# Attention and two feed-forward layers on one core: values by pairs of units, scores of both blocks in one group, sinks placed by VectorE, weight splits held back

## The chip, the cores and the metric

The kernel runs on one core of one Trainium2 chip. The metric is the device time of one execution in microseconds (us), the median of three runs. Engines are named as in the profile: PE is TensorE's matmul side, PEld its weight loads, DVE VectorE, ACT ScalarE, POOL GpSimd, and SP the queue that issues DMAs.

## The reference, cut to what matters

```python
# q, k, v: 2 batches, 8 heads, 768 positions, head size 64, float32; n_sink 4, window 128
scores = scale * np.matmul(q, k.transpose(0, 1, 3, 2))
keep = is_sink | in_window            # the first 4 keys, and the 128 last ones up to the query
a = softmax(np.where(keep, scores, -1e9))
x = np.matmul(a, v)                   # -> 1536 tokens x 512
h = x @ w_in;  x = np.maximum(0.01 * h, h) @ w_out                # 512 -> 2048 -> 512
h = x @ w_in2; x = (h * (1.0 / (1.0 + np.exp(-h)))) @ w_out2      # 512 -> 2048 -> 512
```

## The kernel before

**Attention.** A *unit* is 256 queries (`GT`, a group G) of one pair of heads p; there are 6 groups of 4 units, 24 units, and every unit has two *blocks* of 128 queries, i = 0 and 1. One block of one unit is a *slot*. The groups run in the order of `in_turn`: first the two that begin a sequence (g = 0, units 0 to 7), then the other four (g > 0, units 8 to 23). In the first three groups (units 0 to 11, `whole`) the score matmuls are float32 with a contraction of 64, and the two heads j sit on the upper and the lower half of the array; in the others q and k are cut into float32r parts (`qkh`, `ql`) and the contraction is 128. For a slot, `scores` makes the scores in the PSUM tile `sc`, adds the mask and takes the maximum on DVE (listed as CUSTOM_DVE or ISA, out `P`), and exponentiates on ACT. `normalise` makes the reciprocal of the sum; in units 0 to 7 it builds a scaled identity `by`, in the others it scales `P`. `transposes` turns `P` over on PE (`tr`, or `h` for some) and copies it with ACT into `pT`. With g > 0 the four sink columns go through `psink` (copied by ACT as high part, low part by DVE, and high part again by ACT), are transposed on PE into columns 256 to 383 of the tile `at`, and two ACT copies of 32 rows each (`sink_t<-at`) place them. `values` then multiplies by v (`at<-pT,v`, output of 64 rows for each head) and adds the sinks (`at<-sink_t,sk`); ACT and DVE write the parts `xh` and `xl`.

**Feed-forward.** Each layer has 16 chunks of 128 hidden columns. An *item* is one chunk for some tokens: `emit_h` (12 matmuls into `h`), the nonlinearity on ACT and DVE (`ga`, `gb`, each as a high and a low part), and `emit_y` two items later (`ya` of 256 columns, `y` of 512). While attention runs, 30 items of 256 tokens run beside it; from about 185 us on only items of 512 tokens are left.

**Weights.** Each half of a chunk comes as 64-bit numbers (`wr`, 512 KB) and is made into a high and a low float32r part by two ACT and five DVE instructions (`load_half`: tiles `wb`, then `w` or `we`).

**Order.** All instructions are recorded as operations, and `Recorder.order` places them by a list schedule: durations come from `cost`, and of the operations that could start first the one with the earliest due time is taken. `either` leaves the engine of an operation open; `scaled` could go to ACT, DVE or POOL. Each engine then executes its own row of instructions in the order so written. All engine work is recorded at one source line, so the rows of the profile are told apart by tile names.

Of the kernel before, what the change touches and what calls it, by code (L numbers as in the profile page):

```python
# [36 lines left out]
W_FIRST, W_EVERY = 1, 1.3  # L37

# [8 lines left out]
def f32(ap):  # L47
    return ap.bitcast(F32)


class View:
# [28 lines left out]

    def size(self):
        n = 1
        for a, b in self.box[1:]:
            n *= b - a
        return n
# [28 lines left out]
class Op:  # L114
    def __init__(self, eng, rank):
        self.eng, self.rank = eng, rank
        self.calls, self.cost, self.deps, self.opens, self.users = [], 0, {}, [], []
        self.bytes, self.port, self.mode = 0, False, None

        self.alts = {}  # L120


class Recorder:
# [7 lines left out]
    def __init__(self, tc):  # L131
# [3 lines left out]
        self.after = None  # L135
        for e in self.ENGINES:
            setattr(self, e, _Engine(self, e))
# [13 lines left out]
    def cost(self, eng, name, out, ins, kw):  # L151
        n = out.size() if isinstance(out, View) else 0
        psum = any(isinstance(a, View) and a.tile.pool.psum for a in [out, *ins])
        if eng == "tensor":
            passes = 4 if ins[0].dtype == F32 else 1

            half = name == "matmul" and min(out.box[0][1] - out.box[0][0], ins[0].box[0][1] - ins[0].box[0][0]) <= 64
            if name == "transpose":
                return max(109, n / 2.4)
            return n * passes / 2.4 * (0.5 if half else 1) + (20 if half else 13.3)  # L160
        if name == "dma_start":
            return 0
        if eng == "scalar":
            by = any(isinstance(kw.get(k), View) for k in ("scale", "bias"))
            sparse = isinstance(ins[0], View) and ins[0].tile.tag == "wr"
            return (182 if by else 51 if psum else 93) + n / 1.2 + (95 if "accum_out" in kw else 55 if sparse else 0)
        if eng == "vector":
# [3 lines left out]
            if name == "reciprocal":  # L171
                return 70 + n * 6
            return 68 + n / (0.96 if two or psum else 1.92)
# [15 lines left out]
    def add(self, eng, name, args, kw):  # L189
# [111 lines left out]
    def order(self):  # L301

        for op in self.ops:
            op.need, op.est = len(op.deps), 0.0
            for d in op.deps:
                d.users.append(op)
        self.deadlines()
        free = dict.fromkeys(self.ENGINES, 700.0)
# [43 lines left out]
        while len(done) < len(self.ops):  # L352
# [33 lines left out]
            else:  # L386
                end = free[op.eng] = start + op.cost
                if op.eng == "tensor":

                    end = free[op.eng] = end + (95 if mode is not None and mode != op.mode else 0)  # L390
# [65 lines left out]
def attention_moe(ctx, tc, cfg, ins, out):  # L456
# [35 lines left out]
    def load_half(after=None):  # L492
# [5 lines left out]
        R.after = after  # L498
# [16 lines left out]
        R.after = None  # L515
# [32 lines left out]
    def emit_y(yps, gt, t, layer, c, first, last):  # L548
        cs = slice(c * P, (c + 1) * P)
        with R.group():  # L550
            for j, (a, b) in enumerate(((0, 0), (1, 0), (0, 1))):
                l, r = (wo(t, a)[:, cs], gt[:, b, :]) if layer == 0 else (gt[:, b, cs], wo(t, a))
# [4 lines left out]
    if near:  # L557
        mask = [attn.tile([P, 260], BF16, f"mask{i}") for i in range(4)]
        psink = [attn.tile([P, P], F32, f"psink{i}") for i in range(2)]
        sink_t = [attn.tile([P, GT], F32R, f"sink_t{i}") for i in range(2)]  # L560

# [40 lines left out]
    def load_qk(n):  # L602
# [19 lines left out]
        R.gpsimd.tensor_tensor(ql, raw[:, :, :GT], f32(hi[:, :, :GT]), op=ALU.subtract)  # L622
# [4 lines left out]
    def load_v(n):  # L627
# [7 lines left out]
        if d["g"] > 0 and key not in sinks:  # L635
            sr = attn.tile([P, P + 1], F32, "sr", 2)
            R.sync.dma_start(out=sr, in_=ins["vs"][key])

            sh = attn.tile([P, P], F32R, "sh", 1)
            R.vector.tensor_copy(sh, sr[:, :P])  # L640
            sinks[key] = attn.tile([P, P], F32R, "sk", NP + 1)
            R.vector.scalar_tensor_tensor(sinks[key], in0=f32(sh), scalar=sr[:, P:P + 1], in1=sr[:, :P],
# [5 lines left out]
    def scores(s):  # L648
# [10 lines left out]
        scs = {}  # L659
        if u["whole"]:  # L660

            scs = {j: ps_a.tile([P, 260], F32, "sc", 2) for j in range(2)}
            with R.group():
                for j, sc in scs.items():
# [3 lines left out]
        for j in range(2):  # L668
            if j in scs:
                sc = scs[j]  # L670
            else:
                sc = ps_a.tile([P, 260], F32, "sc", 2)
# [10 lines left out]
    def normalise(s):  # L683
# [5 lines left out]
        if d["u"]["whole"] and d["g"] == 0:  # L689

            d["by"] = attn.tile([P, 2, P], F32, "by", 3)
# [6 lines left out]
        if d["g"] > 0:  # L698
            s0 = 2 * P if i == 0 else P
            src = pt[:, :, s0:s0 + NS]  # L700
            hi, lo, hi2 = (psink[s // 2 % 2][:, o:o + 2 * NS].rearrange("p (j s) -> p j s", j=2)
                           for o in range(32 * i, 32 * i + 6 * NS, 2 * NS))
            R.scalar.activation(hi.bitcast(F32R), src, AF.Copy)
            R.vector.tensor_tensor(lo.bitcast(F32R), src, hi, op=ALU.subtract)
            R.scalar.activation(hi2, hi, AF.Copy)
        R.bias = 0

    def transposes(s):
# [16 lines left out]
        if i == 0:  # L725
            u["pT"] = attn.tile([P, 2, 512], F32, "pT", 2)
# [5 lines left out]
        u["at"] = ps.tile([P, 512], F32, "ya0", 1) if early and s // 2 % 2 else ps_a.tile([P, 512], F32, "at", 1)  # L732
        if g > 0:

            R.tensor.transpose(u["at"][:, 256:384], psink[s // 2 % 2], ident)
            st = u["st"] = sink_t[s // 2 % 2]
            for k in range(2):
                r = slice(32 * k, 32 * k + 32)
                R.scalar.activation(st[r, k * QB:(k + 1) * QB], u["at"][r, 256:384], AF.Copy)

    def values(n):

        u = state.pop(n)
        g, av, v, pT = u["g"], u["at"], u["v"], u["pT"]
        mm = [(1, 128, 384, 0), (0, 0, 128, 0), (2, 384, 512, 128)] if g > 0 else [(0, 128, 384, 0), (1, 384, 512, 128)]
        with R.group():
            if g > 0:
                R.tensor.matmul(av[:, 0:GT], sinks[u["G"] // NG, u["p"]], u["st"], start=True, stop=False)
            for k, (blk, a, e, o) in enumerate(mm):
                for j in range(2):  # L750
                    r = slice(D * j, D * j + D)
                    R.tensor.matmul(av[r, o:o + e - a], v[:, blk, r], pT[:, j, a:e],
                                    start=g == 0 and k == 0, stop=k == len(mm) - 1)
        T, t0 = divmod(u["G"] * GT, 512)
        x = [t[T][:, u["p"], t0:t0 + GT] for t in (xh, xl)]
        R.scalar.activation(x[0], av[:, 0:GT], AF.Copy)
# [294 lines left out]
```

## Time and profile before

| | us |
|---|---|
| median of three runs (lowest, highest) | 629.14 (628.79, 629.53) |
| the profiled execution, its own time | 629.62 |
| span of that execution, first to last instruction | 627.8 |
| PE busy in the span | 616.7 |
| DVE busy | 400.7 |
| ACT busy | 320.7 |
| POOL busy | 29.4 |

The span is what the views below divide up; the execution's own time is 1.8 us longer than its span. A busy PE is not yet PE at its peak, since matmuls are pipelined and their ends are modelled: where PE is compared with itself, the distance between the starts of two rows is used. A matmul in float32 shows as two rows.

### The profile page before, as it was taken

How to read it: one execution, taken by the hardware profiler on the slowest of the kernel's cores; microseconds unless marked ns; L12 is line 12 of the kernel's file. 1: busy time of each engine (PE TensorE's matmuls, PEld its weight loads, DVE VectorE, ACT ScalarE, POOL GpSimd, SP SyncE). 2: the span in 40 equal slices, each digit the busy share in tenths (PEclk: the TensorE clock that was granted, in tenths of full speed). 3: DMA queues.
4: the chain of work that ended last, by engine and by line, in shares of the span. 5: the costliest groups of instructions: out<-in, count | busy, mean ns of one | idle time of the engine just before them, and what ended most of it. 6: DMA issues, size and time to landing. Idle time of an engine off the chain costs nothing.

```text
span 627.8 us, 9200 instructions
## 1 busy us (share of the span) xinstructions
PE 616.7 (98%) x3368; PEld 518.8 (83%) x3368; DVE 400.7 (64%) x984; ACT 320.7 (51%) x789; POOL 29.4 (5%) x44
## 2 busy tenths in 40 slices
PE   7899999999999999999999999999999999999997
PEld 5688888989998888888888888888888888888886
DVE  4998978788696666443646498874554644455254
ACT  5989999999764333332434256454323323332221
POOL 2002013320000000000000000000000000000000
PEclk9999999999999999999999999999999999999999
DMA  8544654331253212020010113220101010000013
GB/s 297 155 167 160 207 173 140 124 102 47 83 190 130 75 62 102 33 68 33 34 66 34 38 66 135 101 101 33 65 4 68 34 34 33 1 0 1 2 67 134
DMA packets 19341, 53.34 MB, mean 85 GB/s; under 512 B 2144, under 2 KB 6752, under 8 KB 19296
## 3 DMA queue, kind: packets, MB, share of 16 engines
q1 hardware_dynamic: 19296, 52.76, 24.6%
q8 instruction: 26, 0.43, 0.3%
q14 instruction: 19, 0.16, 0.1%
HBM read 49.61 MB, written 3.15 MB: 84 GB/s over the span
## 4 chain that ended last, share of the span: by engine, by line
PE 87%; ACT 10%; DVE 2%; issue 1%; DMA 0%; DVEq 0%; ACTq 0%
PE h L441 40%; PE y L441 35%; PE ya L441 5%; ACT P L441 4%; PE sc L441 3%; PE tr L441 2%; PE at L441 2%; ACT pT L441 2%; ACT qkh L441 1%; DVE P L441 1%; ACT psink L441 1%; ACT sink_t L441 1%; ACT ga L441 0%; ACT xh L441 0%; DMA qk<-in_qkd 0%
## 5 line engine op out<-in xcount | busy, mean ns | idle before, releaser
L441 PE MATMUL h<-xh,w 128*128 128x512 f32 (+1 forms) x600 | 157.2, 350 | 0.0
L441 ACT ACTIVATE g<-h 128x512 f32<-128x512 f32 (+1 forms) x111 | 59.6, 537 | 138.5 <-PE h L441 138.5
L441 PEld LDWEIGHTS h<-xh,w 128*128 128x128 f32 x600 | 104.7, 189 | 14.7 <-issue 0.8
L441 DVE TENSOR_TENSOR gb<-g,gb 128x512 fp32r<-128x512 f32 x81 | 55.9, 690 | 77.0 <-ACT g L441 61.2
L441 PE MATMUL h<-xl,w 128*128 128x512 f32 (+1 forms) x300 | 104.0, 347 | 0.0
L441 DVE TENSOR_TENSOR g<-g,h 128x512 f32<-128x512 f32 x48 | 33.0, 687 | 91.6 <-ACT g L441 91.6
L441 DVE SCALAR_TENSOR_TENSOR wb<-wr,wb 128x512 uint32<-128x512 uint32 x128 | 87.7, 689 | 2.8
L441 PE MATMUL h<-xh,we 128*128 128x512 f32 x288 | 88.7, 389 | 0.0
L441 ACT ACTIVATE gb<-h 128x512 fp32r<-128x512 f32 x33 | 19.7, 597 | 100.9 <-PE h L441 100.9
L441 PE MATMUL y<-we,gb 128*128 128x512 f32 x288 | 69.2, 389 | 0.0
L441 PE MATMUL y<-w,gb 128*128 128x512 f32 x288 | 68.9, 389 | 0.0
L441 PEld LDWEIGHTS y<-w,gb 128*128 128x128 f32 x288 | 54.1, 188 | 11.2
L441 PEld LDWEIGHTS y<-we,gb 128*128 128x128 f32 x288 | 54.1, 188 | 11.2
L441 PEld LDWEIGHTS h<-xh,we 128*128 128x128 f32 x288 | 54.1, 188 | 11.1
L441 PEld LDWEIGHTS h<-xl,w 128*128 128x128 f32 x300 | 56.7, 189 | 7.1
L441 ACT ACTIVATE P<-P,sm 128x260 f32<-128x260 f32 (+2 forms) x118 | 56.8, 492 | 7.5 <-DVE sm L441 7.3
L441 PE MATMUL y<-gb,w 128*128 128x512 f32 x252 | 60.5, 389 | 0.0
L441 PE MATMUL h<-xl,we 128*128 128x512 f32 x144 | 56.1, 390 | 0.0
L441 DVE TENSOR_SCALAR wb<-wb 128x512 f32<-128x512 f32 (+1 forms) x128 | 53.6, 424 | 3.6 <-ACT wb L441 2.2
L441 PEld LDWEIGHTS y<-gb,w 128*128 128x128 f32 x252 | 47.3, 188 | 9.8
L441 PE MATMUL ya<-ga,w 128*128 128x256 f32 x360 | 49.6, 286 | 0.0
L441 DVE TENSOR_TENSOR yp<-yp,y 128x512 f32<-128x512 f32 (+1 forms) x61 | 38.0, 673 | 14.7 <-PE y L441 14.7
(72 smaller groups left out, 767.4 us busy)
## 6 DMA issues: line engine op xcount, KB each, us to landing
wr<-in_w SPq DMA_DIRECT2D x64, 512.0 KB, 3.6
qk<-in_qkd SPq DMA_DIRECT2D x12, 644.0 KB, 3.9
v<-in_vd SPq DMA_DIRECT2D x16, 192.0 KB, 2.5
out_y<-yp SPq DMA_DIRECT2D x11, 256.0 KB, 2.1
qk<-in_qkd SPq DMA_DIRECT2D x4, 322.0 KB, 5.7
v<-in_vd SPq DMA_DIRECT2D x8, 128.0 KB, 3.5
qkh<-in_qkd SPq DMA_DIRECT2D x4, 256.0 KB, 6.7
qk<-in_qkd SPq DMA_DIRECT2D x3, 256.0 KB, 3.8
```

Of the source, the lines that this page charges most:

```text
L441: getattr(eng, name)(*[_real(x) for x in a], **{k: _real(x) for k, x in kw.items()})
```

## The change

1. `values` handles two units at once (`us`): their values and sinks stand in one bank `at` (256 columns each) as one uninterrupted group on PE, and `xh` and `xl` are written for both units by one ACT and one DVE instruction. The call moves from every unit to every second one.
2. In the two groups with g = 0, `scores` emits the score matmuls of both blocks of a unit as one group (unit 0 is left in two groups) into one bank for each head. Units 1, 3 and 5 use the bank `ya1` for one head.
3. The sinks are placed by one DVE product of the transposed sinks, read twice, with a 0/1 mask `own`, in place of two ACT copies; the high part goes into `psink` twice with one ACT instruction in place of two.
4. POOL makes masks only: `ql` goes to DVE, and `scaled` has ACT and DVE alone to choose from.
5. The operations of `load_half` may not be scheduled earlier than 16 us (`HOLD`) before their due time.
6. `cost` knows more cases (64-row matmuls, small outputs on ACT, scalars in SBUF on DVE, a slow start of PE, `COLD`), so the schedule is another one throughout.
7. For the last 512 tokens of layer two the last bank is cut into two halves of 256 columns in two banks, and the second half leaves by ACT's DMA queue.
8. Some tiles get other buffer counts: `pT` 3 in place of 2, `by` 2 in place of 3, `sr` 1 in place of 2.

```diff
+COLD = 11000
+HOLD = 16000.0
...
+            return n * passes / 2.4 * (0.5 if half else 1) + (95 if rows <= 64 else 20 if half else 13.3)
...
+            op.split = self.splitting and eng != "sync"
...
-                    ("vector", "tensor_scalar", (out, src, by, None), dict(op0=ALU.mult)),
-                    ("gpsimd", "tensor_scalar", (out, src, by, 1.0), dict(op0=ALU.mult, op1=ALU.mult)))
+                    ("vector", "tensor_scalar", (out, src, by, None), dict(op0=ALU.mult)))
...
+            op.est = max(0.0, op.due - HOLD) if op.split else 0.0
...
-        R.gpsimd.tensor_tensor(ql, raw[:, :, :GT], f32(hi[:, :, :GT]), op=ALU.subtract)
+        R.vector.tensor_tensor(ql, raw[:, :, :GT], f32(hi[:, :, :GT]), op=ALU.subtract)
...
+        if u["whole"] and g == 0:
+            if i == 0:
+                spare = {1: ["ya1", "sc"], 3: ["ya1", "sc"], 5: ["ya1", "sc"]}.get(s // 2, ["sc", "sc"])
+                u["sc"] = [ps_a.tile([P, 512], F32, t, 2) if t == "sc" else ps.tile([P, 512], F32, t, 1) for t in spare]
+            for blocks in ((i,),) if s < 2 else ((0, 1),) if i == 0 else ():
+                with R.group():
+                    for k in blocks:
+                        for j, sc in enumerate(u["sc"]):
+                            r = slice(D * j, D * j + D)
+                            R.tensor.matmul(sc[:, k * P:k * P + P * (k + 1)], u["raw"][r, k * QB:(k + 1) * QB],
+                                            u["raw"][r, GT:GT + P * (k + 1)], start=True, stop=True)
...
-            R.scalar.activation(hi.bitcast(F32R), src, AF.Copy)
+            R.scalar.activation(twice.bitcast(F32R), src.repeat(1, [P, 2, 2, NS]), AF.Copy)
             R.vector.tensor_tensor(lo.bitcast(F32R), src, hi, op=ALU.subtract)
-            R.scalar.activation(hi2, hi, AF.Copy)
...
-            for k in range(2):
-                r = slice(32 * k, 32 * k + 32)
-                R.scalar.activation(st[r, k * QB:(k + 1) * QB], u["at"][r, 256:384], AF.Copy)
+            R.vector.tensor_tensor(st.rearrange("p (k n) -> p k n", k=2), u["at"][:, o:o + P].repeat(1, [P, 2, QB]),
+                                   own.rearrange("p (k n) -> p k n", k=2), op=ALU.mult)
...
+        us = [state.pop(n + k) for k in range(2)]
...
             if g > 0:
-                R.tensor.matmul(av[:, 0:GT], sinks[u["G"] // NG, u["p"]], u["st"], start=True, stop=False)
+                for k, u in enumerate(us):
+                    R.tensor.matmul(av[:, k * GT:(k + 1) * GT], sinks[u["G"] // NG, u["p"]], u["st"],
+                                    start=k == 0, stop=False)
+            for k, u in enumerate(us):
+                for m, (blk, a, e, o) in enumerate(mm):
+                    o += k * GT
+                    for j in range(2):
+                        r = slice(D * j, D * j + D)
+                        R.tensor.matmul(av[r, o:o + e - a], u["v"][:, blk, r], u["pT"][:, j, a:e],
+                                        start=g == 0 and k == m == 0, stop=k == 1 and m == len(mm) - 1)
...
-        R.scalar.activation(x[0], av[:, 0:GT], AF.Copy)
-        R.vector.tensor_tensor(x[1], av[:, 0:GT], f32(x[0]), op=ALU.subtract)
+        both = av.rearrange("p (k n) -> p k n", k=2)
+        R.scalar.activation(x[0], both, AF.Copy)
+        R.vector.tensor_tensor(x[1], both, f32(x[0]), op=ALU.subtract)
...
-                values(b // 2 - 2)
+                if b % 4 == 2:
+                    values(b // 2 - 3)
...
+        ends = layer == 1 and final and T == NT - 1
+        parts = [(c, 0, 512) for c in range(KC - ends)] + ends * [(KC - 1, 0, 256), (KC - 1, 256, 512)]
...
+                (R.scalar if o else R.sync).dma_start(out=out[r0:r0 + P, cols], in_=part)
```

On PE's row of instructions, the stretch around the first values with sinks reads so before (two or three units of g > 0 are under way; `at` is the tile of one unit, and each `at<-pT,v` is 64 rows of output):

```order
L441 MATMUL ya_2_591<-ga_756,w_696 128x256 x6
L441 MATMUL ya_0_604<-ga_756,w_696 128x256 x6
L441 MATMUL at_844<-sink_t_0_129,sk_462 128x256
L441 MATMUL at_844<-pT_779,v_576 64x256 x2
L441 MATMUL at_844<-pT_779,v_576 64x128 x4
L441 MATMUL tr_932<-ident_88,P_753 128x128 x4
L441 MATMUL sc_941<-qk_92 128x260
L441 MATMUL sc_942<-qk_92 128x260
```

The same place of the changed program, where `at_787` is the tile of two units:

```order
L463 MATMUL at_787<-ident_88,psink_0_122 128x128
L463 MATMUL ya_2_904<-ga_817,w_276 128x256 x6
L463 MATMUL sc_916<-qk_92 128x260
L463 MATMUL sc_917<-qk_92 128x260
L463 MATMUL ya_4_924<-ga_817,w_276 128x256 x6
L463 MATMUL at_787<-sink_t_0_807,sk_306 128x256
L463 MATMUL at_787<-sink_t_0_909,sk_493 128x256
L463 MATMUL at_787<-pT_750,v_570 64x256 x2
L463 MATMUL at_787<-pT_750,v_570 64x128 x4
L463 MATMUL at_787<-pT_873,v_725 64x256 x2
L463 MATMUL at_787<-pT_873,v_725 64x128 x4
L463 MATMUL tr_969<-ident_88,P_835 128x128 x4
```

The values of the earlier unit have moved behind those of the later one, so the two runs of 64-row matmuls are one. Over the whole program there are 24 such runs before, 20 of them behind 128-row work and 4 behind scores, and 12 now, 9 and 3; runs of 64-deep score matmuls number 22 before and 15 now, and those that come behind 128-row work 17 and 14.

PE's row at the start, before (`sc` tiles of units 0 and 1, two for each block; `h_187` is a bank used for a transposition):

```order
L441 MATMUL sc_110<-qk_69 128x128
L441 MATMUL sc_111<-qk_69 128x128
L441 MATMUL sc_134<-qk_69 128x256
L441 MATMUL sc_135<-qk_69 128x256
L441 MATMUL sc_153<-qk_69 128x128
L441 MATMUL sc_154<-qk_69 128x128
L441 MATMUL tr_170<-by_159,P_122 128x128 x2
L441 MATMUL sc_181<-qk_69 128x256
L441 MATMUL sc_182<-qk_69 128x256
L441 MATMUL h_187<-by_176,P_144 128x128 x4
```

And in the changed program:

```order
L463 MATMUL sc_110<-qk_69 128x128
L463 MATMUL sc_111<-qk_69 128x128
L463 MATMUL sc_110<-qk_69 128x256
L463 MATMUL sc_111<-qk_69 128x256
L463 MATMUL ya_0_150<-qk_69 128x128
L463 MATMUL sc_151<-qk_69 128x128
L463 MATMUL ya_0_150<-qk_69 128x256
L463 MATMUL sc_151<-qk_69 128x256
L463 MATMUL tr_174<-by_161,P_131 128x128 x2
L463 MATMUL h_189<-by_170,P_143 128x128 x4
```

All scores of two units now stand ahead of the first transposition; the second block of unit 1 has moved up by one place.

DVE's row where the first unit with `ql` is prepared, in the changed program:

```order
L463 TENSOR_TENSOR qkh_828<-qk_69,qkh_828 64x2x388
L463 TENSOR_TENSOR psink_0_122<-P_771,psink_0_122 128x8
L463 TENSOR_TENSOR ql_878<-qk_69,qkh_828 128x512
L463 TENSOR_SCALAR wb_757<-wb_757 128x512
L463 TENSOR_SCALAR sm_836<-sm_836 128x2
L463 CAST sk_897<-sr_820 128x128
L463 ISA P_899,sm_900<-sc_881,mask_0_104 128x260
L463 ISA sm_900 128x1
L463 ISA P_899,sm_900<-sc_882,mask_0_104 128x260
L463 ISA sm_900 128x1
L463 TENSOR_TENSOR sink_t_0_909<-at_787,own_124 128x256
```

Before, neither the `ql` row nor the `sink_t` row stood on DVE; they are new there, 12 and 16 times in all. Counted over the program, DVE also has 43 scalings of `P` in place of 35, ACT 11 `by` in place of 7, and the 4 `by` and 7 scalings of POOL are gone. For the weights, the last half of a chunk is finished on DVE at least 3 items ahead of its first `h` from the 32nd item on; before, that lead was 5 items and more there.

## Rows read from the trace of the kernel before

**Rows 1.** The page: busy time by engine, and the chain that ended last.
```profile
PE 616.7 (98%) x3368; PEld 518.8 (83%) x3368; DVE 400.7 (64%) x984; ACT 320.7 (51%) x789; POOL 29.4 (5%) x44
...
PE 87%; ACT 10%; DVE 2%; issue 1%; DMA 0%; DVEq 0%; ACTq 0%
```

**Rows 2.** Busy time by stretch: length, then each engine with its instructions.
```profile
2.00:13.40 11.40, 9.37 (x36) 6.71 (x36) 5.79 (x38) 5.78 (x23) 2.36 (x12) 1.00 0.97 327
13.40:33.00 19.60, 17.90 (x140) 12.90 (x140) 18.88 (x86) 18.70 (x63) 1.53 (x4) 1.00 0.60 201
...
60.00:100.00 40.00, 39.28 (x334) 34.74 (x334) 34.51 (x133) 39.66 (x126) 7.64 (x6) 1.00 0.53 175
100.00:140.00 40.00, 39.18 (x334) 35.99 (x333) 31.68 (x115) 39.70 (x129) 13.62 (x11) 1.00 0.36 119
...
185.00:624.20 439.20, 439.20 (x1938) 363.67 (x1936) 247.57 (x415) 156.26 (x274) 0.00 (x0) 1.00 0.16 56
```

**Rows 3.** Waits of PE's weight loads, 33 to 185 us: total, times, longest.
```profile
PEld at L441 <- ACT sink_t L441: 1.6, 3, 0.7
PEld sc L441 <- DVE sm L441: 0.9, 2, 0.5
PEld at L441 <- ACT psink L441: 0.5, 1, 0.5
```

**Rows 4.** PE's timeline around the values of two units: start, length.
```profile
31.21 0.87 PE L441 MATMUL at<-pT,v 128*64 128x256 f32 x8
32.01 0.70 PE L441 MATMUL sc<-qkh 64*128 64x256 f32 x4
...
56.70 1.60 PE L441 MATMUL ya<-ga,w 128*128 128x256 f32 x12
58.14 0.28 PE L441 MATMUL at<-sink_t,sk 128*128 128x256 f32 x1
58.35 1.09 PE L441 MATMUL at<-pT,v 128*64 128x256 f32 x12
59.37 0.66 PE L441 MATMUL tr<-ident,P 128*128 128x128 f32 x4
```

**Rows 5.** Groups by line and shape: count, busy us, mean ns, idle before.
```profile
L441 DVE TENSOR_TENSOR gb<-g,gb 128x512 fp32r<-128x512 f32 x81 | 55.9, 690 | 77.0 <-ACT g L441 61.2 <-ACT gb L441 14.8
L441 POOL TENSOR_TENSOR ql<-qk,qkh 128x512 fp32r<-128x512 f32 x12 | 19.3, 1606 | 49.6 <-ACT qkh L441 39.0 <-issue 6.9 <-ACT psink L441 3.7
L441 DVE TENSOR_TENSOR qkh<-qk,qkh 64x776 fp32r<-64x776 f32 x12 | 13.5, 1127 | 1.7 <-ACT qkh L441 1.2
L441 DVE TENSOR_SCALAR P<-P,sm 128x260 f32<-128x260 f32 x35 | 11.7, 358 | 0.4
L441 DVE TENSOR_TENSOR xl<-at,xh 128x256 fp32r<-128x256 f32 x22 | 9.2, 420 | 3.0 <-ACT xh L441 2.7
L441 ACT ACTIVATE xh<-at 128x256 fp32r<-128x256 f32 x22 | 8.3, 377 | 0.7 <-PE at L441 0.7
L441 ACT ACTIVATE sink_t<-at 32x128 fp32r<-32x128 f32 x32 | 8.3, 259 | 0.2
L441 ACT ACTIVATE psink<-psink 128x8 f32<-128x8 f32 x32 | 5.9, 207 | 0.1
L441 ACT ACTIVATE by<-ident,sm 128x128 f32<-128x128 f32 x7 | 2.6, 392 | 0.1
```

**Rows 6.** The last DVE rows, on the timeline from 622 us.
```profile
624.25 0.75 DVE L441 TENSOR_TENSOR yp<-yp,y 128x256 f32<-128x256 f32 x2 [0.67 <-PE y L441]
```

**Rows 7.** DVE's timeline near 106 us.
```profile
106.37 0.96 DVE L441 TENSOR_TENSOR qkh<-qk,qkh 64x776 fp32r<-64x776 f32 x1
```

**Rows 8.** PE's timeline in the opening, 9 to 16 us.
```profile
9.63 2.08 PE L441 MATMUL h<-by,P 128*128 128x128 f32 x8
...
14.94 1.16 PE L441 MATMUL h<-by,P 128*128 128x128 f32 x8
```

**Rows 9.** The chain in order of time: its first work on PE.
```profile
3.20 0.85 PE sc L441 x4
```

More of the change, by code (lines that the diff above doesn't have):

```diff
@@ L135, in __init__ @@
         self.after = None
+        self.splitting = False
         for e in self.ENGINES:
@@ L172, in cost @@
                 return 70 + n * 6
+            if name == "tensor_scalar" and any(isinstance(a, View) for a in ins[1:]):
+                return 128 + n / 1.92
+            if two and not psum and out.box[0][1] - out.box[0][0] <= 64:
+                return 68 + n * 1.19
             return 68 + n / (0.96 if two or psum else 1.92)
@@ L388, in order @@
                 if op.eng == "tensor":
-                    end = free[op.eng] = end + (95 if mode is not None and mode != op.mode else 0)
+                    end += 95 if mode is not None and mode != op.mode else 0
+                    end = free[op.eng] = end + min(op.cost, max(0.0, COLD - start))
                     mode = op.mode
@@ L546, in emit_h, with emit_y @@
         R.vector.tensor_tensor(gt[:, 1, :], g, f32(gt[:, 0, :]), op=ALU.subtract)
-    def emit_y(yps, gt, t, layer, c, first, last):
+    def emit_y(yps, gt, t, layer, c, first, last, cols=slice(0, 512)):
         cs = slice(c * P, (c + 1) * P)
@@ L862, in attention_moe @@
                     R.gpsimd.memset(t, 0.0)
-                for t in sink_t:
-                    for k in (0, P):
-                        R.vector.tensor_copy(t[:, k:k + P], psink[0])
+                R.gpsimd.memset(own, 1.0)
+                for k in range(2):
+                    keep_where(own[:, k * QB:(k + 1) * QB], -32 * k, 1, 0, QB, 0.0)
+                    keep_where(own[:, k * QB:(k + 1) * QB], 32 * k + 31, -1, 0, QB, 0.0)
             while halves[0] < 2 * NA and b >= W_FIRST + halves[0] * W_EVERY:
@@ L922, in fused_h, with fused_y @@
         emit_h(fg[f], wt[c], layer, T, 0, 512)
[L924 removed]
+    def fused_y(f, banks=None):
         layer, c_w, T, first, last, new, final = items[f]
         gt = fg[f]
[L927 to L930 removed]
+        ends = layer == 1 and final and T == NT - 1
+        parts = [(c, 0, 512) for c in range(KC - ends)] + ends * [(KC - 1, 0, 256), (KC - 1, 256, 512)]
+        if first and banks in (None, [0]):
+            yps[:] = [ps.tile([P, 512], F32, "ya0", 1) if o else ps_y.tile([P, 512], F32, f"y{c}") for c, o, _ in parts]
+        for k in banks or range(len(parts)):
+            c, o, e = parts[k]
+            cols = slice(o, e)
+            yp_k = yps[k][:, :e - o]
+            emit_y(yp_k, gt, wt[c_w], layer, c, first, last, cols)
             if not last:
                 continue
[L933 removed]
+            part = yp[T][:, c, cols]
             if new:
[L935 removed]
+                R.scalar.activation(part, yp_k, AF.Copy)
             elif not final:
[L937 removed]
+                R.vector.tensor_tensor(part, part, yp_k, op=ALU.add)
             elif layer == 0:
[L939 removed]
+                R.vector.tensor_tensor(part, part, yp_k, op=ALU.add)
                 R.scalar.activation(xh[T][:, c, :], part, AF.Copy)
@@ L943, in fused_y @@
                 r0 = T * 512 + c * P
-                step = 256 if f == len(items) - 1 and c == KC - 1 else 512
-                for o in range(0, 512, step):
-                    e = slice(o, o + step)
-                    R.vector.tensor_tensor(part[:, e], part[:, e], yps[c][:, e], op=ALU.add)
-                    R.sync.dma_start(out=out[r0:r0 + P, e], in_=part[:, e])
+                R.vector.tensor_tensor(part, part, yp_k, op=ALU.add)
+                (R.scalar if o else R.sync).dma_start(out=out[r0:r0 + P, cols], in_=part)
     for f in range(len(items)):
@@ L956, in attention_moe @@
             fused_y(f - 2)
-    for c in range(KC):
+    for k in range(KC + 1):
         for f in (len(items) - 2, len(items) - 1):
-            fused_y(f, [c])
+            fused_y(f, [k])
     R.issue(ctx)
```

86 lines of the change are left out of this document (42 added, 44 removed).

## The prediction, made before the run

> **What bounds the kernel now.** I read the page first, for the engines' shares and the chain that ended last: PE is busy in 98% of the span and holds 87% of the chain, ACT 10% [rows 1]. So PE is the limit almost everywhere, and the question is where it isn't. The table by stretch answers that. From 185 to 624.2 us PE is busy without a gap, 439.2 of 439.2 us, and DVE and ACT are far from full (247.6 and 156.3) [rows 2]. Nothing can be won there that doesn't take matmuls away, and the change takes none away. In the attention stretch from 60 to 140 us PE is busy 78.5 of 80 us, but ACT is busy 79.4 of 80 and DVE 66.2 [rows 2]: PE and ACT are both full, and whatever ACT does late, PE waits for. The waits of the weight loads say for what: 1.6 us for the sink copies of ACT, 0.9 us for the softmax on DVE that frees the score banks, 0.5 us for the `psink` copies of ACT, 3.0 us in all between 33 and 185 us [rows 3]. Last comes the opening, where neither is full: 9.37 of 11.4 us of PE from 2 us on, then 17.9 of 19.6 [rows 2].
>
> A busy PE may still stand still inside a row, so I then looked at the distances between starts on PE's timeline. Twelve `ya` matmuls of 256 columns take from 56.70 to 58.14, so 0.12 us each. The sink matmul behind them has the same 256 columns, but the first 64-row matmul starts 0.21 us after it: going into the 64-row shape costs 0.09 us [rows 4]. The run of twelve rows lasts until 59.37, 1.02 us; the run of eight rows at 31.21 lasts 0.80 us until 32.01. The four extra rows are two 128-column matmuls and cost 0.22, 0.11 us each. A 256-column one is then 0.22, and the eight rows (two of each) should take 0.66; the missing 0.14 us goes into the first load in the new shape and the way out of it [rows 4]. So one run of values costs 0.09 us on the way in and 0.14 us inside and on the way out.
>
> **The change, part by part.** The sum is made against the profiled execution's own 629.62 us, which is 0.48 above the median of 629.14.
>
> *Values by pairs.* Runs go from 24 to 12, and those entered from 128-row work from 20 to 9. That is 11 x 0.09 = 1.0 us and 12 x 0.14 = 1.7 us, 2.7 us of PE's time, in the stretch where PE is full. No row shows two units in one run, so the lower bound is 0 (the shape is paid for again at each unit), the upper 2.7. I take 2.7: the eight and twelve rows show no extra step between matmuls of one shape.
>
> *Scores of both blocks in one group.* Entries from 128-row work go from 17 to 14: 3 x 0.09 = 0.3 us. Each score matmul keeps its own cost.
>
> *Sinks and `psink`.* ACT loses 32 copies of 0.259 and 32 of 0.207 us, 14.9 us. 24 `xh` copies of 0.377 become 12 of twice the columns, which I count as no saving. Four `by` come from POOL at 0.392: 1.6 us more. So ACT is rid of some 13 us [rows 5], most of it between 45 and 160 us, and is no longer full there. PE's 1.6 and 0.5 us of waits for ACT's sink work are then waits for DVE, which makes the product. All 3.0 us of [rows 3] could go (upper bound) or stay (lower bound 0). I take 1.5, because DVE gets work, which the next point adds up.
>
> *DVE.* It gets 12 `ql` at 0.69 (the price of a 512-column two-input row), 16 sink products at 0.42 and 8 scalings at 0.358, 17.9 us, and loses 1.8 us because 24 `xl` of 0.42 become 12 of 0.69 [rows 5]. That is 16.1 us, hidden as long as DVE keeps up with PE: from 60 to 140 us it has 13.8 us free [rows 2], and some three quarters of the new work, 12 us, falls there. That fits, barely. Two things loosen it. Rows back to back overlap: two 256-column adds take 0.75 us together [rows 6], not twice 0.42 [rows 5]. And the high-part subtraction `qkh` takes 0.96 us where it runs alone [rows 7] but 1.127 on the mean [rows 5], since POOL's `ql` runs beside it: 12 x 0.17 = 2.0 us come back. I cost it at nothing; the price if the cover fails is the first rival.
>
> *Weight splits held back.* Work is only moved, within stretches where DVE and ACT are not full. From the 32nd item on the splits end at least 3 items ahead of use, and an item of 24 matmuls at 0.227 (439.2 us over 1938 rows [rows 2]) is 5.4 us, so 16 us stay as cover. Their loads stand on SP's queue with the loads of q, k and v, and one that waits for a buffer would hold those up; they stand where a buffer is due, so nothing is added. Costed at 0.
>
> *The end.* Now the two last adds run one after the other behind the last matmul, 0.75 us [rows 6]; with two banks only one, 0.42, follows it. Six matmuls of 512 columns become twelve of 256, and 2 x 0.12 against 0.227 is 0.013 x 6 = 0.08 us more. The gain is 0.25 us. No row shows an output sent by ACT's queue; I take it to be as quick as SP's (if it costs as much as the second add, the gain is gone, 0).
>
> *The opening.* ACT has more `by` to make (1.6 us) but fewer splits at the start, and PE's first transposition comes behind two units' scores. Up to 1.6 us could be lost, and up to PE's idle time there be won, 0.8 us (11.4 - 9.37 = 2.0, less the 1.2 before its first matmul at 3.2 [rows 9]) and 1.7 us [rows 2], so 2.5. I take 0, as the two bounds lie on both sides of it.
>
> The sum is 2.7 + 0.3 + 1.5 + 0.25 = 4.75 us. 629.62 - 4.75 = 624.87, and as much below the median: **624.4 us**. Deeper `pT`, fewer `by` and `sr` buffers are in the order already.
>
> **The rivals.**
>
> *A wait for the pair (slower).* The group of two units starts only when the last of its four `pT` and two sink tiles is there, and the two new sink products stand in the queue of a DVE that is 95% busy: 66.2 + 12 - 2.0 of 80 us. Behind PE's wait everything of PE is queued. If each of the 12 pairs waits 0.7 us, as long as the longest wait for a sink copy [rows 3], that is 8.4 us; with the 1.5 us of waits that I let stand included in it, 624.4 + 6.9 = 631.3. It decides from about 0.5 us a pair on: 12 x 0.52 = 6.25, which is 1.5 that stay and the 4.75 won. For it speaks that ACT at 99% caused just such waits; against it, that they came 6 times in all [rows 3], and that behind the transposition of the first pair's later sinks PE has 2.0 us of other work (two times six `ya` at 0.12, and scores of about 0.6 [rows 4]) before their product is wanted.
> [...]
>
> *The grouping pays nothing.* The shape is paid for again inside the group, and the waits stay at 3.0 us with DVE in ACT's place. Then 0.3 and 0.25 us are left: 628.6. Nothing in [rows 4] speaks for it, but nothing shows the opposite either.
>
> [...]
> [...]
>
> **How the numbers follow.** My forecast gets 0.52, the pair's wait 0.13, the grouping that pays nothing 0.15, the short opening 0.20. A measurement of this kernel tells about 0.2%, 1.26 us, from no change, so "same" is 627.88 to 630.40. Faster: 0.52, 0.20, and 0.06 of the third, 0.78. Slower: 0.11 of the pair's wait. Same: the remaining 0.02 and 0.09, 0.11. Terms at their bounds give 624.4 - 1.5 = 622.9 and 624.4 + 1.5 = 625.9 for the waits alone, and 2.7 more if the pairs save nothing. The range of 8 in 10 goes from 621.3 to 628.3: it takes in the short opening and most of the third rival, and leaves out the pair's wait.
>
> **What would show it.** In the changed profile: a run of 24 rows of values that lasts about 1.9 us (two of 1.02 less 0.14); ACT clearly below 79 of 80 us between 60 and 140, DVE above 75; waits for sink work on DVE of 1 to 2 us in total; PE without a gap from the end of attention on, shifted forward by some 4.5 us; one 256-column add behind the last matmul. The forecast is wrong if PE's weight loads wait for DVE for more than 3 us in sum, if the first `h` starts over a microsecond later or earlier than before, or if PE shows gaps at the first use of a chunk.

## The result, and the profile after

The changed kernel takes 623.67 us (median of 4 executions, 622.55 to 624.05) against 629.34 for the kernel before on the same chip; the ratio is 0.9904 with an interval of 0.9887 to 0.9921. Run again in a later set it took 623.46 (622.56 to 624.36). The forecast was 624.4. The profiled execution took 623.91 us, its span is 622.2 us; before, 629.62 and 627.8.

The page, busy time by engine and the chain that ended last:

```profile
PE 610.6 (98%) x3374; PEld 518.1 (83%) x3374; DVE 401.2 (64%) x1004; ACT 312.6 (50%) x716; POOL 5.0 (1%) x26
...
PE 84%; DVE 7%; ACT 6%; DMA 2%; SPq 1%; issue 1%; ACTq 0%
```

ACT lost 8.1 us and POOL 24.4, while DVE, which took over their work, is where it was [rows 1]. Busy time by stretch (length, then PE, PEld, DVE, ACT, POOL):

```profile
2.00:13.40 11.40, 9.75 (x50) 7.22 (x50) 6.76 (x38) 5.63 (x21) 3.62 (x17) 1.00 0.97 317
13.40:33.00 19.60, 16.63 (x142) 13.25 (x142) 18.90 (x91) 19.45 (x68) 0.00 (x0) 1.00 0.58 205
60.00:100.00 40.00, 38.64 (x340) 35.85 (x341) 36.15 (x143) 36.53 (x107) 0.00 (x0) 1.00 0.53 173
100.00:140.00 40.00, 39.82 (x358) 37.73 (x357) 37.25 (x139) 38.42 (x110) 0.00 (x0) 1.00 0.35 114
185.00:619.00 434.00, 434.00 (x1921) 359.43 (x1919) 241.97 (x420) 157.71 (x271) 0.00 (x0) 1.00 0.16 57
```

From 60 to 140 us ACT is down to 74.95 of 80 us, and DVE up to 73.40 [rows 2]. PE stands idle for 1.54 us there, exactly as long as before: what it waits for has changed, not how long. From 185 us on PE is full, as before; the whole gain is made earlier, save for the end. Waits of PE's weight loads, 33 to 185 us:

```profile
PEld tr L463 <- ACT pT L463: 2.3, 3, 1.3
...
PEld sc L463 <- DVE sm L463: 0.5, 1, 0.5
```

The waits for sink work of [rows 3] are gone; a new one, 1.3 us long, is for ACT's copy into `pT`. Around the first pair of values with sinks, and in the opening, PE's timeline reads:

```profile
8.47 1.91 PE L463 MATMUL h<-by,P 128*128 128x128 f32 x8
10.31 0.93 PE L463 MATMUL sc<-qk 64*128 64x128 f32 x8
11.17 0.71 PE L463 MATMUL tr<-by,P 128*128 128x128 f32 x4
11.71 1.06 PE L463 MATMUL h<-by,P 128*128 128x128 f32 x8
...
16.28 0.87 PE L463 MATMUL at<-pT,v 128*64 128x256 f32 x8 [1.07 <-ACT pT L463]
...
60.70 0.39 PE L463 MATMUL at<-sink_t,sk 128*128 128x256 f32 x2
61.02 1.96 PE L463 MATMUL at<-pT,v 128*64 128x256 f32 x24
62.91 0.66 PE L463 MATMUL tr<-ident,P 128*128 128x128 f32 x4
```

24 rows of values last 1.89 us (61.02 to 62.91); two runs of 1.02 [rows 4] are 2.04, so 0.15 is saved inside. At 16.28 the second half of a pair waits for its `pT`, 1.07 us in the row. The scores of both blocks take 0.86 us in one group (10.31 to 11.17). The same four matmuls in two groups, in the kernel before, take 0.42 us (16.03 to 16.45) and 0.63 (17.90 to 18.53):

```profile
16.03 0.49 PE L441 MATMUL sc<-qk 64*128 64x128 f32 x4
16.45 0.71 PE L441 MATMUL tr<-by,P 128*128 128x128 f32 x4
...
17.90 0.70 PE L441 MATMUL sc<-qk 64*128 64x256 f32 x4
18.53 1.16 PE L441 MATMUL h<-by,P 128*128 128x128 f32 x8
```

Eight rows into `h` take 1.84 us at 8.47 (to 10.31) and 0.99 at 11.71 (to 12.70, where the next scores start): the longer durations of PE's first rows end around 10 us here, between 11.7 and 14.9 before [rows 8], though the granted clock is printed as 1.00 throughout. No row shows what makes them longer, and the same order doesn't end them at the same time: in the profile of the second set the same score group takes 1.58 us (10.41 to 11.99) in place of 0.86, so they last there until about 12 us:

```profile
10.41 1.65 PE L463 MATMUL sc<-qk 64*128 64x128 f32 x8
11.99 0.74 PE L463 MATMUL tr<-by,P 128*128 128x128 f32 x4
```

The last rows of the changed kernel, on DVE and on ACT's queue:

```profile
619.04 0.42 DVE L463 TENSOR_TENSOR yp<-yp,ya 128x256 f32<-128x256 f32 x1 [0.29 <-PE ya L463]
619.49 0.37 ACTq L463 DMA_DIRECT2D out_y<-yp  x1
```

Where the 5.6 us of the span came from is told by the distances between starts on PE, added up by the kind of row over attention, before and after: values and sink matmuls 26.56 to 24.90 (the stall of 1.24 us at 16.28 is in it), 64-deep scores 18.95 to 18.09, transpositions of `P` with `by` 14.76 to 13.73 and with `ident` 14.44 to 13.62, scores with `qkh` 13.55 to 12.72, `psink` 1.21 to 0.54; the `ya` rows went from 45.33 to 46.11, since the new wait stands behind them. A wait is counted with the row ahead of it, so these sums hold PE's own time and its waits. The first `h` of 256 columns starts at 28.01 us (26.36 before), the third at 38.0 (40.0), the 11th at 86.3 (88.7), the 21st at 140.3 (145.8), the 30th at 172.3 (177.6): 2.0 us are won before the third `h` and 3.1 between the 11th and the 21st.

### The profile page after: what moved, and what is told of

The parts are those of the page before. It is cut to its first block, busy times and chain, and to the rows that moved or that the text cites. A ratio compares the mean times of both kernels' runs of the same rounds, so it can differ in the third digit from the quotient of the medians.

```text
span 622.2 us, 9107 instructions
## 1 busy us (share of the span) xinstructions
PE 610.6 (98%) x3374; PEld 518.1 (83%) x3374; DVE 401.2 (64%) x1004; ACT 312.6 (50%) x716; POOL 5.0 (1%) x26
## 4 chain that ended last, share of the span: by engine, by line
PE 84%; DVE 7%; ACT 6%; DMA 2%; SPq 1%; issue 1%; ACTq 0%
PE h L463 40%; PE y L463 35%; PE ya L463 5%; ACT P L463 3%; DVE P L463 2%; PE at L463 2%; PE tr L463 1%; DMA wr<-in_w 1%; DVE wb L463 1%; PE sc L463 1%; ACT pT L463 1%; SPq L463 1%; DVE qkh L463 1%; DMA sr<-in_vs 1%; ACT qkh L463 1%
## 5 line engine op out<-in xcount | busy, mean ns | idle before, releaser
L463 PE MATMUL h<-xh,we 128*128 128x512 f32 x288 | 88.7, 389 | 0.0
L463 DVE SCALAR_TENSOR_TENSOR wb<-wr,wb 128x512 uint32<-128x512 uint32 x128 | 85.8, 685 | 1.0
L463 PE MATMUL y<-w,gb 128*128 128x512 f32 (+1 forms) x288 | 68.2, 387 | 0.0
L463 PEld LDWEIGHTS y<-we,gb 128*128 128x128 f32 x288 | 54.1, 188 | 11.2
L463 PEld LDWEIGHTS h<-xh,we 128*128 128x128 f32 x288 | 54.1, 188 | 11.2
L463 PEld LDWEIGHTS ya<-ga,w 128*128 128x128 f32 x360 | 45.4, 190 | 2.0 <-issue 1.4
```

Of the source, the lines that this page charges most:

```text
L463: getattr(eng, name)(*[_real(x) for x in a], **{k: _real(x) for k, x in kw.items()})
```

## The experiments

Each is an edit of the changed kernel. "Places kept" means that the order is computed as in the changed kernel and only then altered. Medians stand against 623.5 us, between the two medians of the changed kernel.

**Values one unit at a time, planned anew.** Each unit has its own group on PE and its own `xh` and `xl`; the bank is still that of the pair.

```diff
...
-                if b % 4 == 2:
-                    values(b // 2 - 3)
+                values(b // 2 - 2)
```

> Values one unit at a time again, in the banks of the changed kernel, planned anew; xh and xl are written for each unit. My prediction's step (runs of one shape cost 0.09 us on the way in and 0.14 inside and out): 12 more runs, 2.7 us slower, 626.4. If the wait inside the first pair (1.24 us at 16.28) goes with the pairs: 1.2 to 1.6 us slower, 625.1. Rival (the grouping pays nothing): within 0.5 us of the changed kernel.

Measured: 626.84 us (626.01 to 627.70), ratio to before 0.9953 [0.9937, 0.9970]: 3.4 us slower than the changed kernel in the same set. Added up as above, values and sink matmuls take 26.41 us against 24.58 there, and 0.92 of the 24.58 is the stall at 16 us: 2.75 us of PE's own time. The grouping pays, at the size of the step. The rest is waits, which this order has in other places: in the opening four values wait for their `pT` (2.6 and 2.5 us in all), and two waits for `xh` are new, since both units share a bank. The stall at 73 us of the changed kernel, told below, is gone. Long waits for `pT` do not come from taking the values unit by unit: the kernel before does so too, and its values wait for `pT` once in the opening, 0.3 us. Waits of PE's weight loads, 0 to 33 us and 33 to 185 us:

```profile
PEld ya L463 <- ACT pT L463: 2.6, 2, 1.3
PEld at L463 <- ACT pT L463: 2.5, 2, 1.3
...
PEld at L463 <- ACT xh L463: 1.1, 2, 0.6
```

**A sink matmul between the two units of a pair, places kept.**

```diff
-                for k, u in enumerate(us):
-                    R.tensor.matmul(av[:, k * GT:(k + 1) * GT], sinks[...], u["st"], start=k == 0, stop=False)
+                R.tensor.matmul(av[:, 0:GT], sinks[...], us[0]["st"], start=True, stop=False)
             for k, u in enumerate(us):
+                if g > 0 and k == 1:
+                    R.tensor.matmul(av[:, GT:2 * GT], sinks[...], u["st"], start=False, stop=False)
```

> Each of the 8 pairs with sinks takes its matmuls in the order sink, values, sink, values in place of sink, sink, values, values; nothing else is changed. My theory (the gain is PE's own time at the changes of shape): every pair pays one more way in (0.09 us) and one more way out (0.14), 8 x 0.23 = 1.8 us, so 625.5 against 623.7, and the 24 rows become two runs of 12 with a sink row of some 0.21 us between them. Rival (the gain comes from less waiting, or from ACT's relief): within 0.4 us of the changed kernel.

Measured: 625.09 us (624.16 to 627.03), ratio 0.9930 [0.9907, 0.9954]: 1.6 us slower, near the 1.8. PE's timeline:

```profile
60.39 0.28 PE L463 MATMUL at<-sink_t,sk 128*128 128x256 f32 x1
60.60 1.09 PE L463 MATMUL at<-pT,v 128*64 128x256 f32 x12
61.62 0.39 PE L463 MATMUL at<-sink_t,sk 128*128 128x256 f32 x1
61.93 1.09 PE L463 MATMUL at<-pT,v 128*64 128x256 f32 x12
62.95 0.66 PE L463 MATMUL tr<-ident,P 128*128 128x128 f32 x4
```

From the first sink to the transposition it is 2.56 us, in the changed kernel 2.21 (60.70 to 62.91): 0.35 for one break, more than the 0.23. The sink in the middle takes 0.31 and not 0.21, so coming back out of the 64-row shape costs some 0.1 by itself. Eight breaks of 0.35 make 2.8 us, and the value and sink rows are longer by that much in sum (24.90 to 27.76 us); that the time rose by 1.6 only, near the forecast, is partly luck, since the stall of over 1.2 us at 73 us, told below, is missing from this run's profile.

**Scores of both blocks apart, places kept but for the second block.** The group of a unit is cut behind the first block, and the second (`rest_of`) follows the next 128-row operation on PE.

```diff
+            for name, a, kw in op.calls[:cut]:
+                getattr(eng, name)(...)
+            if op.eng == "tensor" and all(op.mode):
+                rest_of()
```

> In the seven units 1 to 7 of g = 0 the scores of the second block come one 128-row operation later on PE than those of the first; every other row keeps its place. The trace of the changed kernel has 0.86 us for the four score matmuls of a unit in one group, before it had 0.42 and 0.63 in two. My theory (PE's time counts in the opening too): six or seven times 0.19 inside and 0.09 on the way in, 1.1 to 1.9 us slower, 625.2. What I had predicted: only the ways in, 0.3 us to 0.6. Rival (ACT, busy 19.45 of 19.6 us from 13.4 to 33 us, sets the opening): within 0.4 us. [...]

Measured: 626.51 us (625.64 to 627.30), ratio 0.9946 [0.9926, 0.9966]: 3.0 us slower, above both. PE's timeline of the third unit:

```profile
11.21 0.49 PE L472 MATMUL sc<-qk 64*128 64x128 f32 x4
12.20 0.71 PE L472 MATMUL tr<-by,P 128*128 128x128 f32 x4 [0.50 <-ACT pT L472]
12.84 0.70 PE L467 MATMUL sc<-qk 64*128 64x256 f32 x4
13.47 1.16 PE L472 MATMUL h<-by,P 128*128 128x128 f32 x8
```

The 64-deep score rows sum to 20.87 us, 2.9 more than in the second profile of the changed kernel (17.93). Six of the seven units come apart (at 14.56 the four matmuls of one unit still stand together and take 0.86 us); at 0.19 each, the difference between 0.42 + 0.63 and 0.86, that is 1.1 us of PE's own time. Most of the rest is waits behind these rows, such as the 0.50 us at 12.20. Eight rows into `h` take 1.63 us at 9.58 and 1.09 at 13.47: the longer durations end between 9.6 and 11.2 us, within the 10 to 12 of the changed kernel, so the grouping shows no part in their ending earlier than before.

**Sinks placed by ACT again (14 of the 16), places kept.**

```diff
+                R.ops[-1].instead = ("scalar", [("activation", (st[32 * k:32 * k + 32, ...], u["at"][...], AF.Copy), {})
+                                                for k in range(2)])
```

> 14 of the 16 sink products of DVE are two ACT copies of 32 rows each again (28 x 0.26 = 7.3 us back on ACT, 5.9 us off DVE), each in the same place of the order. My prediction's step (waits of 3.0 us, half of them gone with ACT's relief): 1.5 us slower, 625.2, with waits of PE's weight loads for sink copies back. Rival, by the changed trace (PE's stalls from 33 to 185 us sum to 2.6 us after and 2.8 before): the waits only changed their names, and this is within 0.4 us of the changed kernel.

Measured: 627.88 us (627.00 to 629.85), ratio 0.9967 [0.9950, 0.9984]: 4.4 us slower. PE's weight loads, 33 to 185 us, wait mostly for other work than sinks (0.2 us for `sink_t`):

```profile
PEld tr L463 <- ACT pT L463: 4.9, 8, 1.1
PEld sc L463 <- DVE sm L463: 1.6, 3, 0.8
```

**The same copies, with the order planned for them.** The edit puts them into the program as recorded, in place of the product.

> As the run before it that put 14 of the 16 sink products back on ACT as two copies each, but the order is planned with these copies in it, in place of keeping the places of an order that was planned for DVE (that run lost some 3.5 to 4 us). Theory A (ACT's load is what costs: it has 5 us free of 80 between 60 and 140 us, and the copies are 7.3): 2.5 to 4 us slower than the changed kernel again, 626.2 to 627.7. Theory B (that run's loss came from copies put into a row that had no place for them): 0 to 1 us slower, 623.7 to 624.7.

Measured: 625.53 us (625.00 to 626.33), ratio 0.9927 [0.9912, 0.9942]: 2.0 us slower, between the two theories. So some 2.4 us of the other run's loss came from copies without a place in the order. That the remaining 2.0 us are the worth of ACT's relief is not shown: PE's idle time from 60 to 140 us is 1.42 us here, no more than the 1.54 of the changed kernel (3.65 in the run with places kept), and orders of the same instructions differ by up to 1.8 us, as the last runs below show.

**`ql` made by POOL, places kept.**

```diff
+        R.ops[-1].instead = ("gpsimd", R.ops[-1].calls)
```

> The 12 subtractions that make ql go back to POOL, each in the same place of the order. My theory: POOL gets 19 us, DVE loses 8 us and gets 2 us back as longer qkh rows (1.1 us each in place of 0.96); DVE isn't what PE waits for, so within 0.4 us of the changed kernel. Rival (POOL's reading holds up DVE, and the softmax on DVE frees the score banks late): over 1 us slower, with more waits of PE for sm. Rival the other way (DVE at 73 of 80 us holds PE up): over 0.5 us faster.

Measured: 625.38 us (624.68 to 626.24), ratio 0.9929 [0.9909, 0.9949]: 1.9 us slower; my theory of no effect falls. DVE's groups (count, busy us, mean ns), in the changed kernel:

```profile
L463 DVE TENSOR_SCALAR P<-P,sm 128x260 f32<-128x260 f32 x43 | 14.0, 351 | 0.4
L463 DVE TENSOR_TENSOR qkh<-qk,qkh 64x776 fp32r<-64x776 f32 x12 | 11.6, 965 | 2.5 <-ACT qkh L463 2.2
...
L463 DVE TENSOR_TENSOR psink<-P,psink 128x8 fp32r<-128x8 f32 x32 | 4.8, 161 | 1.5 <-ACT psink L463 1.4
```

and in this run:

```profile
L463 DVE TENSOR_TENSOR qkh<-qk,qkh 64x776 fp32r<-64x776 f32 x12 | 15.8, 1317 | 2.1 <-ACT qkh L463 1.8
L463 DVE TENSOR_SCALAR P<-P,sm 128x260 f32<-128x260 f32 x43 | 15.5, 386 | 0.4
...
L463 DVE TENSOR_TENSOR psink<-P,psink 128x8 fp32r<-128x8 f32 x32 | 6.9, 224 | 1.3 <-ACT psink L463 1.2
```

`qkh` is 4.2 us longer in sum, `psink` 2.0, the scalings 1.5, the two-column `sm` rows 1.3 and `ga` 1.1 (0.419 to 0.456 us, 30 rows): 10.1 us, for 12 `ql` of POOL of 1.504 us, 18.0 us. Taking 8.3 us of `ql` off DVE left it busier by 3.1 us (404.3 against 401.2).

By the starts and ends of the rows, all of the 10.1 us lies in 20 rows that stand beside a `ql` of POOL: 8 of the 12 `qkh` take 1.493 us on the mean there and the other 4 0.965, 3 of the 32 `psink` 0.845 and the others 0.160. Rows of DVE that read PSUM are not longer: 6 maxima (`P<-sc,mask`) take 0.420 us beside a `ql` and 0.421 elsewhere, 3 `sink_t` 0.420 and 0.417. In both pairs of lines below the row that started second is the long one. In the first POOL is 0.01 us ahead, and DVE's row takes 2.10 us in place of 0.96; in the second DVE is ahead, and POOL's takes 2.08 in place of 1.28:

```profile
90.40 1.28 POOL L463 TENSOR_TENSOR ql<-qk,qkh 128x512 fp32r<-128x512 f32 x1 [4.93 <-ACT qkh L463]
90.41 2.10 DVE L463 TENSOR_TENSOR qkh<-qk,qkh 64x776 fp32r<-64x776 f32 x1
...
72.80 0.96 DVE L463 TENSOR_TENSOR qkh<-qk,qkh 64x776 fp32r<-64x776 f32 x1 [1.27 <-ACT qkh L463]
72.85 2.08 POOL L463 TENSOR_TENSOR ql<-qk,qkh 128x512 fp32r<-128x512 f32 x1 [16.00 <-ACT qkh L463]
```

PE meets it as waits for DVE, 33 to 185 us; in the changed kernel the first is 0.5 us, once, and the second is not listed:

```profile
PEld sc L463 <- DVE sm L463: 1.9, 4, 0.8
...
PEld at L463 <- DVE psink L463: 0.6, 2, 0.4
```

**No hold on the splits.** `HOLD = 1.0e9`.

> The splits of the weights may start whenever their data is there (the hold of 16 us before the due time is lifted); the order is planned anew. What I had predicted: work is only moved, 0, so within 0.5 us of the changed kernel (623.7). Rival (early splits take ACT and DVE away from the softmax of the opening, where ACT is busy 19.45 of 19.6 us): 1 to 3 us slower, with the loss before 40 us and the first h over 1 us earlier or later.

Measured: 623.96 us (623.21 to 624.38), ratio 0.9900 [0.9884, 0.9916]. No difference, as predicted; the first `h` starts at 28.2 us.

**The old end.** `fused_y` as before: one bank of 512 columns, two adds, both halves sent by SP.

> The last bank is one of 512 columns again, with two adds behind the last matmul and both halves sent by SP. My theory: 0.25 us slower (0.75 us of adds in place of 0.42, less 0.08 of matmuls); the profile's span from the last matmul's end grows by 0.3 to 0.4 us. Rival (ACT's queue sends no sooner): no difference.

Measured: 624.47 us (622.94 to 624.67), ratio 0.9905 [0.9889, 0.9921]: inconclusive by the times. From the 30th `h` to the end of the span it is 450.2 us, before too (177.6 to 627.8), and 449.9 in the changed kernel: 0.3 us. The other runs with the new end have 449.9 as well, but for the one without the hold, which has 450.2.

**The planner's durations of before, and no slow start.**

```diff
-COLD = 11000
+COLD = 0
...
-            return n * passes / 2.4 * (0.5 if half else 1) + (95 if rows <= 64 else 20 if half else 13.3)
+            return n * passes / 2.4 * (0.5 if half else 1) + (20 if half else 13.3)
...
```

> The planner's durations are those of before (without the 64-row, the small-output and the SBUF-scalar cases, and without the slow start); the instructions are the same, in another order. Theory (the gain is in the instructions: shapes, ACT's relief, POOL's absence): within 0.7 us of the changed kernel. Rival (a large part of the gain is the better planned order): 2 to 4 us slower, with PE idle over 3 us between 60 and 140 us, where the changed kernel has 1.54.

Measured: 621.95 us (620.86 to 622.97), ratio 0.9869 [0.9849, 0.9888]: neither theory; 1.6 us faster than the changed kernel. PE's idle time from 60 to 140 us falls from 1.54 to 0.16 us:

```profile
60.00:100.00 40.00, 39.91 (x352) 37.03 (x351) 36.69 (x146) 38.29 (x110) 0.00 (x0) 1.00 0.52 164
100.00:140.00 40.00, 39.93 (x359) 37.92 (x359) 37.88 (x140) 39.08 (x114) 0.00 (x0) 1.00 0.36 113
```

**The two halves of it, and the changed kernel again.** `COLD = 0` with the new durations; the old durations with `COLD = 11000`.

> The changed kernel once more, as the base for the other three of this call: 623.7 us, within 0.5. Two theories on its longest stall between 33 and 185 us (1.26 us at 73.21, a transposition behind ACT's copy of pT, which stood behind a qkh copy 5.7 us after its load was issued, with a 512 KB weight load issued 1.2 us behind that load): if the load's landing varies, the stall is shorter than 0.4 us or absent in some executions, as in the runs where the order there was the same; if it is the order alone, it is there with over 1 us each time.

> The changed kernel without the planner's slow start (COLD at 0), the new durations kept. The run with the old durations and without the slow start took 621.95 us, 1.7 us less than the changed kernel. If the slow start is what makes the order worse, this is 1.2 to 2 us faster than the changed kernel, with the first h before 27.6 us; if the new durations are (64-row matmuls at 95 ns, small ACT outputs, scalings), it is within 0.5 us of it.

> The other half: the planner's durations of before, with the slow start. If the durations are what makes the order worse, this is near 622, 1.2 to 2 us faster than the changed kernel; if the slow start is, within 0.5 us of it. If neither half alone gives it, both runs stand at 623 to 624, and the gain belongs to one order that came out well by chance.

Measured: 623.46 us (622.56 to 624.36), ratio 0.9898 [0.9878, 0.9917]; 621.62 (621.14 to 621.92), 0.9868 [0.9846, 0.9890]; 622.09 (621.75 to 622.34), 0.9875 [0.9854, 0.9897]. Either half gives the whole gain, so it is neither the slow start nor one duration: the three other orders agree within 0.5 us, and that of the changed kernel is 1.4 to 1.8 us worse. All three gain between the third `h` and the 11th, 48.25 us in the changed kernel (38.0 to 86.3), 46.8, 46.8 and 45.9 in these; with the slow start left out alone, as much again is gained before the third `h` (36.6 against 38.0). With the slow start left out alone, the kernel is the fastest of all, 7.9 us under the kernel before.

What the changed order has there is a stall at 73 us. ACT and PE in the changed kernel's first profile:

```profile
71.39 1.28 ACT L463 ACTIVATE qkh<-qk 128x1288 fp32r<-128x1288 f32 x1 [1.01 <-issue]
72.57 0.58 ACT L463 ACTIVATE pT<-tr 128x512 f32<-128x512 f32 x1
...
73.21 0.66 PE L463 MATMUL tr<-ident,P 128*128 128x128 f32 x4 [1.09 <-ACT pT L463]
```

The transposition wants the bank `tr`, which `pT` must first empty, and `pT` stands on ACT behind the copy `qkh` of a unit that just arrives. The load of that unit, issued at 65.70 (KB, us to landing), and in the run with the sink in between, with the same places there, at 65.75:

```profile
qk<-in_qkd SPq DMA_DIRECT2D x1, 644.0 KB, 5.6
```

```profile
qk<-in_qkd SPq DMA_DIRECT2D x1, 644.0 KB, 4.3
```

The stall of over 1.2 us is there at 5.6 us of landing (the changed kernel, both times); at 5.4 and 5.3 us (`ql` by POOL, and sinks by ACT, places kept) it is 1.1 and 0.9, and at 4.3 and 4.4 (sink in between, old end) it is gone. So the theory that the landing varies holds, but over 1 us came back in each profile of the unaltered kernel. In the changed order the weight load of 512 KB is issued 1.2 us behind this load; with the old durations it comes 3.9 us behind (68.99 after 65.12), and the load of q and k lands in 4.0 us. That the weight load slows it is not shown: with the slow start alone left out it is issued 0.5 us behind (65.27 after 64.75), and yet the copy `qkh` starts 4.4 us after its load's issue, with no stall; and with the old durations alone the load takes 5.05 us (issued at 65.05) though no weight load is issued between 60 us and 69.41. The order without the hold has no such stall either and gains nothing, and with the old end, in the same order, the 11th `h` comes at 86.5 us without the stall. So a stall less is not yet a gain, and what makes the changed order worse than its three neighbours stays open.

## Why the prediction was right, step by step

- **Values by pairs, 2.7 us.** Right in mechanism and size: undone, it costs 2.75 us of PE's time, and 3.4 in all. Between the two kernels these rows fall by 1.66 us, 2.9 without the stall at 16.28. That stall is the wait of the first rival, but it comes in one pair of 12, 1.24 us: the rival stayed out.
- **Scores in one group, 0.3 us.** Mis-sized. "Each score matmul keeps its own cost" was the wrong sentence: in one group four of them take 0.86 us at 10.31, where the same four in two groups take 0.42 and 0.63 in the kernel before, 0.19 more, or 1.3 us for seven units. Undone for six of them, the group costs 3.0 us in all, with the waits that come behind; between the two kernels the score rows differ by 0.86 us.
- **Waits, 1.5 of 3.0.** The sink waits went entirely and DVE caused none in their place, but PE's idle time between 60 and 140 us is the same 1.54 us. ACT's rows sum to 12.4 us less (380.2 to 367.8), near the 13 of the prediction, but its busy time fell by 8.1 only, since rows back to back overlap (367.8 us of rows in 312.6 us of busy time). What this relief is worth is not settled: with the sinks back on ACT and planned anew the time is 2.0 us longer, but orders of the same instructions differ by nearly as much. With other durations, the same instructions leave 0.16 us idle. The step took the waits as a matter of load; they were one of order as well.
- **DVE hidden, cost 0.** Right, and both reasons given hold. DVE came to 73.4 of 80 us, not above 75. The overlap of rows is the larger reason: from 60 to 140 us DVE's rows sum to 11.8 us more than before (80.5 to 92.3), close to the 12 of the prediction, and its busy time grew by 7.2. The absence of POOL's `ql` gives back 1.9 us in `qkh`, as predicted, and 0.4 in `psink` (5.2 to 4.8). In the changed order `ql` by POOL makes DVE's rows on SBUF 10.1 us longer, for POOL's 18.0 us. It is not the whole of the 18.0: the rows that read PSUM go on beside POOL (0.420 us, 0.421 elsewhere), and where DVE is ahead POOL's row is the long one (2.08 us in place of 1.28). The kernel's own planner keeps POOL's work and DVE's rows on SBUF apart, and before, with an order planned so, `qkh` was at 1.127 us and not 1.317.
- **Splits held back, 0.** Right: without the hold the time is the same.
- **The end, 0.25.** 0.3 us by the spans, though one run with the new end has the length of the old; the times don't settle it.
- **The opening, 0.** The first `h` comes 1.65 us later, which the prediction named as a sign against it, but more of attention is done first: 148 of its rows on PE stand ahead of the first `h`, 132 before. Ahead of the third `h` they are as many in both kernels, 196, and it comes 2.0 us earlier. So the opening won about 2 us, most of the 2.5 that the prediction set as its upper bound. With the scores apart the third `h` comes at 40.8, so the group carries it. A part of the longer durations of PE's first rows in it doesn't show: in the second profile of the changed kernel they last some 2 us longer, and the third `h` comes at 37.75, no later than in the first. What ends them stays open. No run shows a cause of the short opening to which the prediction gives 0.20: PE's idle time from 2 to 33 us rose from 3.73 us to 4.62, and what came 2.0 us earlier is the third `h`.

So the total came out right by terms that were too small (scores, opening) and one that the order took back (waits): the main step, the values, was right as a mechanism, but that the sum lies within 0.8 us is in part luck. The prices of undoing don't add up to the gain: 3.4, 3.0, 2.0, 1.9 and 0.3 make 10.6 us, less 1.6 for the order 9.0, against 5.7 measured (6.0 in the later set). Two were taken with places kept in an order planned for other work, where such a loss was twice that of a new plan (4.4 and 2.0); how much of the rest is shared between them stays open.

## What to carry to other kernels

Put matmuls of one tile shape together: here 12 more runs of values cost 2.75 us of PE's time, 0.35 us for a break with a sink in it, and that price stood in the distances between starts on PE, not in the busy share (98% in both kernels). Where a planner writes the order, an edit's worth is known only to about 1.5 us until a few neighbouring orders have been timed: change its costs and run again before taking a stall for the edit's own. Look in the order for a copy that may wait for a load and stands ahead of one that frees PE's bank: here that place cost up to 1.3 us of PE's time, though taking it away did not by itself make the kernel faster. Before giving work on SBUF to POOL, add up what it does to DVE: here 18.0 us of POOL's made DVE's rows on SBUF 10.1 us longer, while rows of DVE that read PSUM kept their 0.42 us beside it.

## What the runs showed of the hardware

PE's first rows were longer than rows of the same shape later (eight rows into `h` 1.84 us at 8.47 and 0.99 at 11.71), until about 10 us in one profile of the changed kernel, about 12 in another, and past 11.7 before, while the granted clock was printed as 1.00. Beside a subtraction of POOL on SBUF (1.28 us where it isn't held up), DVE's rows on SBUF took longer: `qkh` rows up to 2.10 us in place of 0.96, `psink` rows of 8 columns 0.845 us on the mean in place of 0.160, scalings of one SBUF input 0.648 in place of 0.351; rows that read PSUM kept their 0.42 us. The same load of 644 KB, at the same place of the order, took between 4.3 and 5.6 us to land.
